# A rank-20 product for the second MLP matmul, with sixteen kept sums

## The chip, the cores and the metric

The program runs on one core of a Trainium2 chip. A core has TensorE (PE in the profile, its weight loads PEld), VectorE (DVE), ScalarE (ACT), GpSimd (POOL) and SyncE (SP, which here only starts transfers), each with its own in-order queue of instructions. The metric is device time in microseconds, the median of several runs.

## The reference

Four batches of 768 tokens pass a gated linear attention with 8 heads of width 48, then a two-layer MLP with an ELU. Everything is single precision for the kernel; the MLP weights arrive as 64-bit floats.

```python
f = 1.0 / (1.0 + np.exp(-f_logit))
for t in range(S):
    state = f[:, :, t, :, None] * state + np.einsum('bhd,bhe->bhde', k[:, :, t], v[:, :, t])
    y[:, :, t] = np.einsum('bhd,bhde->bhe', q[:, :, t], state)
x = y.transpose(0, 2, 1, 3).reshape(B * S, H * D)      # 3072 x 384
h = x @ w_in                                            # 384 x 2048
g = np.where(h > 0.0, h, np.exp(np.minimum(h, 0.0)) - 1.0)
out = g @ w_out                                         # 2048 x 384
```

## The kernel before

The 3072 tokens are cut into 12 units of 256 (two blocks of 128). The work of a unit in the MLP is 16 steps T (unit m has T = 16m to 16m+15); two steps make a pair P, and a pair handles 256 of the 2048 hidden features, so a unit has 8 pairs j = 0 to 7. The main loop writes out the order by hand, step by step, in the order in which it is then queued on every engine:

- At an even T, `up7` (L891 ff.) makes the first product for pair P. It saves one product in eight with sums of weights and inputs (`mix`, `blend`, both on GpSimd), and writes two banks of PSUM, `pa` and `pb`, which are one buffer each: the next pair's `pb` products cannot start before VectorE has read this pair's. Eight instructions go to `pa`, twelve to `pb`. Between the two groups ScalarE copies one block of `pa` (L908, `u1`), VectorE adds it to two others (L910, `hh`), and then VectorE does the ELU of the pair before (`elu`, L955).
- At an odd T, `joined` (L920 ff.) adds the rest from `pb` with three VectorE additions (L923), then ScalarE runs Relu and Exp over the 128x512 result (L933, L934).
- `elu(P)` runs two steps after `joined(P)`, and from its 128x512 result GpSimd makes four sums of 128x128 blocks (L965).
- At an odd T, `down(P-2)` (L969 ff.) multiplies with `w_out`. Here too seven products of half width (192 columns) replace eight, with four blocks of hidden values, four sums of them (`sums`), four blocks of `w_out` and four combinations of them made once (`combine`, L861 ff., VectorE, steps 16 to 31). They accumulate over the unit's 8 pairs in four PSUM banks m0 to m3. A single-precision matmul is two instructions in the trace, so a pair's second product is 14 instructions of 192 columns. When j = 7 is done, one ScalarE copy and five VectorE additions (L1013, L1014) turn the seven sums into the output, and SyncE stores it.
- Unit 0 does both products plainly, since the combinations are not ready: 8 instructions of 384 columns for a pair (L978).

The attention of later units lies between these steps, put there with `at_step`. For unit u it is, in steps counted from the start of unit u-1: at T = 2 transposes of k; at T = 5 `both(u)`, with products into banks a0, a1 and then scores into m3 and m0 (the step's `down` is left out and made up at T = 7), the masks (L721) and the state additions (L694) on VectorE; at T = 9 `outputs`; at T = 11 `carried`; at T = 13 `blend` on GpSimd. The gates of the unit after come at T = 9, 11, 13 and 15: a scan (L630) and a reciprocal (L635) on VectorE, products with k and q on GpSimd (L625).

The kernel also rereads the weights in 32 pieces during units 3 to 10 and checks their range (`check`, L601 ff.): two VectorE reductions (L607) for each, at T = 6, 10, 14 and 2. One small matmul group on bank m3 at T = 4 (16 matmuls) and one on a0 at T = 22 (5) are there for no result (`warm`).

Of the kernel before, what the change touches and what calls it, by code (L numbers as in the profile page):

```python
# [8 lines left out]
FP32 = mybir.dt.float32  # L9
# [4 lines left out]
ALU = mybir.AluOpType  # L14
# [339 lines left out]


@with_exitstack
def fast(ctx: ExitStack, tc: tile.TileContext, q, k, v, f_logit, w_in, w_out, out, flag, outer):
# [33 lines left out]
    NP = NFT // 2  # L391
    DH = DM // 2
    DIRECT = 1
    LAG = 2
    AHEAD = 7
    WA = 1
    F1 = 3
    W0 = 3
    SMALL = 16
    MORE = 5  # L400
    RR = 2
# [7 lines left out]
    MX = 10  # L409
    CB = 16  # L410
    BL1 = 13
    LIMIT = 2.0**80

    FULL = (slice(0, 64), slice(64, 128))
# [85 lines left out]

    even_v = cst.tile([128, NW, NKT, 64], FP32, name="even_v")
    nc.gpsimd.memset(even_v[:], 0.0)
    padded_v = cst.tile([128, NW, 2 * NKT, 3 * PAD], FP32, name="padded_v")
    nc.gpsimd.memset(padded_v[:], 0.0)
    padded_s = cst.tile([128, NC - 1, NKT, 3 * PAD], FP32, name="padded_s")
    nc.gpsimd.memset(padded_s[:], 0.0)
    between = cst.tile([128, NW, HP], FP32, name="between")
# [9 lines left out]
    if wide:  # L517
        combos = [area[:, i].bitcast(FP32).rearrange("p (n f) -> p n f", f=DH) for i in (5, 6, 0, 1)]
    else:
        apart = cst.tile([128, 4, NP, DH], FP32, name="combos")  # L520
        combos = [apart[:, i] for i in range(4)]

# [78 lines left out]
    def check(n):  # L601

        if not wide:
            return
        hi = again.pop(n)[:].bitcast(FP32)[:, 1::2]
        for i, op in enumerate((ALU.min, ALU.max)):
            nc.vector.tensor_reduce(  # L607
                out=spans[:, i, n : n + 1], in_=hi, axis=mybir.AxisListType.X, op=op, apply_absolute_value=True
            )

# [149 lines left out]
    def carried(u):  # L760
# [3 lines left out]
        for w in range(NW):  # L764
            for p in range(HP):
                for b in range(2):
# [3 lines left out]
                    for r in range(2):  # L770
# [4 lines left out]
                        )  # L775
        x = xts[u] = sb.tile([128, HP + 1, U], FP32, tag="xt", name=f"xt{u}", bufs=3)
        to = x[:, 0:HP].rearrange("n p (w b i) -> n b w p i", b=2, i=C)
# [9 lines left out]
    def first_outputs(part):  # L787
# [32 lines left out]
        if part == 0:  # L820
            for b in range(2):
                nc.scalar.copy(between[:, :, 0:NKT], first_y[b][:, :, :, 0])
            return
        x = xts[0] = sb.tile([128, HP + 1, U], FP32, tag="xt", name="xt0", bufs=3)
        to = x[:, 0:NKT].rearrange("n p (w b i) -> n b w p i", b=2, i=C)
# [6 lines left out]
    def at_step(step, *todo):  # L832
        plan.setdefault(step, []).extend(todo)
# [27 lines left out]
    def combine():  # L861

        b = [[wo[:, i::2, h * DH : (h + 1) * DH] for h in range(2)] for i in range(2)]
        t = combos
        for n in range(0, NP, 2):
            for to, x, y in (
                (t[0], b[0][1], b[0][0]), (t[1], b[1][1], t[0]), (t[2], b[1][1], b[0][1]), (t[3], b[1][0], t[1]),
            ):
                nc.vector.tensor_tensor(
                    out=to[:, n : n + 2], in0=x[:, n : n + 2], in1=y[:, n : n + 2], op=ALU.subtract  # L870
                )
                yield

# [78 lines left out]
    def elu(P):  # L952
        m, j = order[P]
        g = gs[P]
        nc.vector.scalar_tensor_tensor(  # L955
            out=g[:], in0=g[:], scalar=-1.0, in1=phs.pop(P), op0=ALU.add, op1=ALU.max
        )
        if m >= DIRECT:
            s = ss[P] = sb.tile([128, 4, 128], FP32, tag="sums", name=f"sums{m}_{j}", bufs=3)
            a = [[g[:, i, t * 128 : (t + 1) * 128] for i in range(2)] for t in range(2)]  # L960
            for i, x, y, op in (
                (0, a[1][0], a[1][1], ALU.add), (2, a[0][0], a[1][0], ALU.subtract),
                (1, s[:, 0], a[0][0], ALU.subtract), (3, a[0][1], s[:, 1], ALU.subtract),
            ):
                nc.gpsimd.tensor_tensor(out=s[:, i], in0=x, in1=y, op=op)  # L965

    left = []

    def down(P):  # L969
        m, j = order[P]  # L970
        if j == 0:
            pms[m] = [ps.tile([128, DM], FP32, tag=f"m{i + (m < DIRECT)}", name=f"psM{m}_{i}") for i in range(NW if m < DIRECT else 4)]
        pm, g = pms[m], gs.pop(P)
        ends = dict(start=(j == 0), stop=(j == NP - 1))
        if m < DIRECT:
            for i in range(2):
# [12 lines left out]
            return  # L989
        s = ss.pop(P)  # L990
        a = [[g[:, i, t * 128 : (t + 1) * 128] for i in range(2)] for t in range(2)]
        b = [[wo[:, 2 * j + i, h * DH : (h + 1) * DH] for h in range(2)] for i in range(2)]
        c = [combos[i][:, j] for i in range(4)]

        todo = [
            (0, 0, a[0][0], b[0][0]), (3, 0, a[0][1], b[1][0]), (0, 1, s[:, 1], c[1]),
            (1, 0, s[:, 0], c[0]), (1, 1, s[:, 2], c[2]), (2, 1, a[1][1], c[3]), (2, 0, s[:, 3], b[1][1]),
        ]
        if j == 0:
            todo = todo[3:] + todo[:3]  # L1000
        for bank, half, x, y in todo:
            first = j == 0 and (bank, half) in ((0, 0), (3, 0), (1, 0), (2, 1))
            nc.tensor.matmul(  # L1003
                pm[bank][:, half * DH : (half + 1) * DH], lhsT=x, rhs=y,
                start=first, stop=(j == NP - 1), skip_group_check=True,
            )
        if j == NP - 1:
            p = [[pm[i][:, h * DH : (h + 1) * DH] for h in range(2)] for i in range(4)]
            o = (outer if (NU - m) % 2 else sb).tile([128, 2, DM], FP32, tag="o", name=f"o{m}", bufs=1)
            u2 = sb.tile([128, DH], FP32, tag="u2", name=f"u2_{m}", bufs=1)  # L1010
            u43 = sb.tile([128, 2, DH], FP32, tag="u43", name=f"u43_{m}", bufs=1)
            flat = o[:].rearrange("p t f -> p (t f)")
            add = lambda to, x, y: nc.vector.tensor_tensor(out=to, in0=x, in1=y, op=ALU.add)  # L1013
            (nc.vector.tensor_copy if m == NU - 1 else nc.scalar.copy)(u2[:], p[0][0])  # L1014
            add(flat[:, 0:DH], p[3][0], u2[:])
            add(u2[:], p[0][1], u2[:])
            add(u43[:], pm[1][:].rearrange("p (h f) -> p h f", h=2), u2[:].unsqueeze(1).broadcast_to([128, 2, DH]))
            add(flat[:, 3 * DH :], p[1][0], u43[:, 1])
            add(flat[:, DH : 3 * DH], pm[2][:], u43[:].rearrange("p h f -> p (h f)"))
            def store(*queues):  # L1020
                for t in range(2):
                    for h in ((1, 0) if t else (0, 1)):
                        queues[t].dma_start(
                            out=out[m * U + t * 128 : m * U + (t + 1) * 128, h * DH : (h + 1) * DH],
                            in_=o[:, t, h * DH : (h + 1) * DH],
                        )

            if m == NU - 1:
                left.append(store)
            else:  # L1030
                store(nc.sync, nc.sync)
            del pms[m]

    low = cst.tile([128, 1], FP32, name="low")

    def finish_flag(part):
        if wide and not part:
            ok = fine[:, 0, 0:1]
            nc.vector.tensor_reduce(out=spans[:, 0, 0:1], in_=spans[:, 0], axis=mybir.AxisListType.X, op=ALU.min)
            nc.vector.tensor_reduce(out=spans[:, 1, 0:1], in_=spans[:, 1], axis=mybir.AxisListType.X, op=ALU.max)  # L1040
            for i, op, limit in ((0, ALU.is_ge, 1.125 * 2.0**-15), (1, ALU.is_lt, 1.875 * 2.0**16)):
                nc.vector.scalar_tensor_tensor(
                    out=ok, in0=spans[:, i, 0:1], scalar=limit, in1=ok, op0=op, op1=ALU.mult
                )
        if not part:
            nc.vector.tensor_reduce(
                out=low[:], in_=fine[:].rearrange("p a c -> p (a c)"), axis=mybir.AxisListType.X, op=ALU.min
            )
            return
        pf = ps.tile([128, 1], FP32, tag="a0", name="psF")  # L1050
        nc.tensor.matmul(pf[0:1, :], lhsT=low[:], rhs=causal[:, W - 1 : W], start=True, stop=True)
        nc.vector.tensor_copy(flag[:], pf[0:1, :])
# [97 lines left out]
    at_step(4, lambda: warm(0, "m3", SMALL))  # L1150
    at_step(22, lambda: warm(0, "a0", MORE))
    attention(1, (), A1)
# [3 lines left out]
    weights = combine()  # L1156
    for n in range(NFT):
        at_step(CB + n, lambda: next(weights))
# [17 lines left out]
    for T in range(NU * NFT):  # L1176
# [14 lines left out]
        for n in later.pop(T, ()):  # L1191
            split(n)
            if n not in (A1[2], A1[2] + 1):
                lower(n)
    elu(NU * NP - 1)
    for P in range(NU * NP - LAG, NU * NP):
# [51 lines left out]
```

## Time and profile before

| what | before |
|---|---|
| median of 3 runs | 562.21 us (561.53 to 562.24) |
| profiled execution, its own time | 563.12 us |
| its span from first to last instruction | 561.4 us |
| PE busy | 542.9 us, 97% |
| DVE busy | 407.5 us, 73% |
| POOL busy | 293.3 us, 52% |
| ACT busy | 228.1 us, 41% |
| one unit, 311.55 to 354.74 us | 43.19 us |

In the profile a group of instructions is a line of the kernel, an engine, an operation and its tiles; then come how often it ran, its busy time, the mean length of one, and the idle time of the engine just before it with what ended that. The time from one instruction's start to the next one's is less than the length of one, because instructions of an engine overlap at their ends.

### The profile page before, as it was taken

How to read it: one execution, taken by the hardware profiler on the slowest of the kernel's cores; microseconds unless marked ns; L12 is line 12 of the kernel's file. 1: busy time of each engine (PE TensorE's matmuls, PEld its weight loads, DVE VectorE, ACT ScalarE, POOL GpSimd, SP SyncE). 2: the span in 40 equal slices, each digit the busy share in tenths (PEclk: the TensorE clock that was granted, in tenths of full speed). 3: DMA queues.
4: the chain of work that ended last, by engine and by line, in shares of the span. 5: the costliest groups of instructions: out<-in, count | busy, mean ns of one | idle time of the engine just before them, and what ended most of it. 6: DMA issues, size and time to landing. Idle time of an engine off the chain costs nothing.

```text
span 561.4 us, 15627 instructions
## 1 busy us (share of the span) xinstructions
PE 542.9 (97%) x6358; PEld 507.9 (90%) x6358; DVE 407.5 (73%) x804; ACT 228.1 (41%) x442; POOL 293.3 (52%) x567
## 2 busy tenths in 40 slices
PE   6889989999999999999999999999999999999996
PEld 2466768999999999999999999999999999999995
DVE  8888989786675785785785785786687777735553
ACT  3288752443343434434344343343333343333331
POOL 6600797475375375465366267257258348325332
PEclk9999989999999999999999999999999999999999
DMA  8999971024025216207307307207307302301101
GB/s 198 233 266 247 276 184 43 3 48 123 2 48 149 61 26 182 77 18 189 81 9 189 87 10 190 85 9 191 86 9 185 93 9 71 87 5 33 31 2 34
DMA packets 39474, 54.30 MB, mean 97 GB/s; under 512 B 4032, under 2 KB 29216, under 8 KB 39392
## 3 DMA queue, kind: packets, MB, share of 16 engines
q1 hardware_dynamic: 38592, 52.61, 36.3%
q8 instruction: 52, 0.85, 0.6%
q10 hardware_dynamic: 800, 0.59, 0.5%
q14 instruction: 30, 0.25, 0.2%
HBM read 45.02 MB, written 4.72 MB: 89 GB/s over the span
## 4 chain that ended last, share of the span: by engine, by line
PE 85%; DMA 7%; DVE 3%; ACT 2%; issue 1%; SPq 1%; POOL 0%; ACTq 0%; DVEq 0%; POOLq 0%
PE psH L901 39%; PE psM L1003 36%; DMA area<-in_moe_w_in_dram 5%; DMA area<-in_moe_w_out_dram 2%; PE psY L751 2%; PE psY L771 2%; PE psU_a L736 2%; PE psS L713 2%; ACT area L577 1%; PE psT L673 1%; PE psM L978 1%; DVE bits L567 1%; DVE gg L955 0%; DVE wi L585 0%; DVE state L694 0%
## 5 line engine op out<-in xcount | busy, mean ns | idle before, releaser
L901 PE MATMUL psH<-xt,wi 128*128 128x128 f32 (+1 forms) x1056 | 195.9, 295 | 0.0
L965 POOL TENSOR_TENSOR sums<-gg 128x128 f32<-128x128 f32 x176 | 77.6, 462 | 209.6 <-DVE gg L955 190.9
L933 ACT ACTIVATE gg<-hh 128x512 f32<-128x512 f32 x88 | 55.5, 631 | 252.9 <-DVE hh L923 111.9
L901 PEld LDWEIGHTS psH<-xt,wi 128*128 128x128 f32 x1056 | 150.1, 192 | 1.6
L901 PE MATMUL psH<-xt,area 128*128 128x128 f32 x704 | 122.0, 275 | 2.0 <-DVE gg L955 2.0
L901 PEld LDWEIGHTS psH<-xt,area 128*128 128x128 f32 x704 | 106.9, 192 | 6.8 <-DVE gg L955 2.2
L910 DVE TENSOR_TENSOR hh<-psH,u 128x256 f32<-128x256 f32 x88 | 37.0, 421 | 99.6 <-ACT u L908 99.6
L1003 PE MATMUL psM<-area,sums 128*128 128x192 f32 x528 | 102.1, 326 | 0.1
L1003 PEld LDWEIGHTS psM<-area,sums 128*128 128x128 f32 x528 | 88.0, 190 | 0.2 <-issue 0.2
L1003 PE MATMUL psM<-wo,gg 128*128 128x192 f32 x352 | 73.9, 332 | 0.0
L955 DVE SCALAR_TENSOR_TENSOR gg<-gg,hh 128x512 f32<-128x512 f32 x88 | 63.3, 720 | 1.5 <-ACT gg L934 1.5
L635 DVE RECIPROCAL f<-f 128x256 f32<-128x256 f32 x36 | 62.8, 1747 | 1.1
L934 ACT ACTIVATE gg<-gg 128x512 f32<-128x512 f32 x96 | 60.5, 631 | 3.0
L1003 PEld LDWEIGHTS psM<-wo,gg 128*128 128x128 f32 x352 | 56.3, 190 | 1.4
L923 DVE TENSOR_TENSOR hh<-psH,u43h 128x256 f32<-128x256 f32 (+1 forms) x176 | 54.7, 353 | 3.0
L965 POOL TENSOR_TENSOR sums<-gg,sums 128x128 f32<-128x128 f32 x88 | 46.8, 532 | 6.9
L625 POOL TENSOR_TENSOR q<-q,f 128x256 f32<-128x256 f32 x48 | 39.7, 829 | 18.1 <-DMA area<-in_moe_w_in_dram 15.1
L625 POOL TENSOR_TENSOR k<-k,f 128x256 f32<-128x256 f32 x48 | 39.7, 830 | 9.5 <-DMA f<-f 6.7
L923 DVE TENSOR_TENSOR u43h<-psH,hh 128x256 f32<-128x256 f32 x88 | 37.0, 421 | 9.2 <-PE psH L901 8.5
L965 POOL TENSOR_TENSOR sums<-sums,gg 128x128 f32<-128x128 f32 x88 | 43.4, 493 | 0.0
L1003 PE MATMUL psM<-area,gg 128*128 128x192 f32 x176 | 43.0, 326 | 0.0
L1003 PE MATMUL psM<-wo,sums 128*128 128x192 f32 x176 | 43.0, 326 | 0.0
(100 smaller groups left out, 648.7 us busy)
## 6 DMA issues: line engine op xcount, KB each, us to landing
area<-in_moe_w_out_dram SPq DMA_DIRECT2D x8, 768.0 KB, 11.0
again<-in_moe_w_in_dram SPq DMA_DIRECT2D x16, 384.0 KB, 4.2
again<-in_moe_w_out_dram SPq DMA_DIRECT2D x16, 384.0 KB, 3.7
k<-in_k_dram SPq DMA_DIRECT2D x12, 384.0 KB, 4.5
q<-in_q_dram SPq DMA_DIRECT2D x12, 384.0 KB, 5.6
v<-in_v_dram SPq DMA_DIRECT2D x12, 384.0 KB, 6.0
area<-in_moe_w_in_dram SPq DMA_DIRECT2D x8, 576.0 KB, 9.4
out_dram<-o SPq DMA_DIRECT2D x42, 96.0 KB, 2.0
```

The lines of the kernel that those rows point to most:

```text
L625: e.tensor_tensor(out=t[n][:, p], in0=t[n][:, p], in1=t["f"][:, p, "kq".index(n)], op=ALU.mult)
L635: nc.vector.reciprocal(f[:, p, 1], f[:, p, 0])
L713: nc.tensor.matmul(pc[r][FULL[b], w, p], lhsT=t["k"][FULL[r], p, cols], rhs=t["q"][FULL[r], p, cols], start=True, stop=True,)
L736: nc.tensor.matmul(pu[b][FULL[r], w, p], lhsT=kn[FULL[b], p, w, FULL[r]], rhs=vs[u % NB][FULL[b], w, PAD + h * D : PAD + (h + 1) * D], sta ...
L901: nc.tensor.matmul(to, lhsT=lhs, rhs=rhs, start=(n == 0), stop=True, skip_group_check=True)
L910: add = lambda to, x, y: nc.vector.tensor_tensor(out=to, in0=x, in1=y, op=ALU.add)
L923: add = lambda to, x, y: nc.vector.tensor_tensor(out=to, in0=x, in1=y, op=ALU.add)
L933: nc.scalar.activation(g[:], h, AF.Relu, scale=-1.0)
L934: nc.scalar.activation(g[:], g[:], AF.Exp, scale=-1.0)
L955: nc.vector.scalar_tensor_tensor(out=g[:], in0=g[:], scalar=-1.0, in1=phs.pop(P), op0=ALU.add, op1=ALU.max)
L965: nc.gpsimd.tensor_tensor(out=s[:, i], in0=x, in1=y, op=op)
L1003: nc.tensor.matmul(pm[bank][:, half * DH : (half + 1) * DH], lhsT=x, rhs=y, start=first, stop=(j == NP - 1), skip_group_check=True,)
```

## The change

The second product for two pairs (four tiles of 128 hidden features, two token blocks, three column blocks of 128) is made with 20 products of 128 columns in place of 2 times 7 of 192. The 20 products go to 16 sums c0 to c15, four to a PSUM bank. They need 14 sums of hidden blocks a0 to a13 and 14 combinations b0 to b13 of weight blocks. Names in the tables: x0 to x7 are hidden blocks (4 features tiles by 2 token blocks), w0 to w11 blocks of `w_out`, o0 to o5 blocks of the output.

- `elu`: after an even pair GpSimd makes a0 to a3 (4 additions); after an odd pair VectorE makes a5, a7, a10 (3), and GpSimd the other 8.
- `down`: an even pair issues the first 10 products, an odd pair the other 10. In the last unit the last two pairs' 20 are issued together, by bank.
- `ended`: after a unit ScalarE copies three banks (128x512 each) and one block of the fourth, and VectorE does 22 additions of 128x128. They are put out four at the end of each step (`SPREAD`), from step 3 of the next unit; the store follows. In the last unit they run at once, four of them on GpSimd.
- `combine`: 20 operations of 128x512, 18 on GpSimd and 2 on VectorE, at steps 18 to 37.
- Unit 1 does its second product plainly.
- `check`: Square and Relu on ScalarE with their row sums, in place of the two VectorE reductions.
- Smaller: the group of 5 `warm` matmuls goes and the other has 15; three padded tiles become one (`spare`), cleared by one instruction; the MLP inputs have two buffers in place of three.

```diff
-    SMALL = 16
-    MORE = 5
+    PLAIN = 2
+    SPREAD = 4
+    SMALL = 15
-    CB = 16
+    CB = 18
...
+SUMS_OF_TWO = table(
+    "a0 x0 - x1, a1 a0 - x4, a2 x5 + a1, a3 x0 - x4, "
+)
+SUMS_SOON = table(
+    "a5 x2 - x6, a7 x4 + x2, a10 x2 - x7, "
+)
+SUMS_OF_FOUR = table(
+    "a12 a0 + x7, a4 x6 - x7, a6 x5 + a4, a9 x4 + x6, a8 x1 + x2, a8 a8 - x3, a13 x0 + x2, a11 x3 - x7, "
+)
+PRODUCTS = (
+    table(
+        "x4 b10 c0, x5 w5 c11, x1 b12 c14, a0 b1 c2, a1 b8 c1, a2 w3 c8, a3 b6 c7, x7 b9 c10, x2 b5 c4, "
+        "a5 w6 c9, "
+    ),
+    table(
+        "a7 b3 c3, a10 b4 c5, a12 b7 c6, a4 b13 c11, a6 b0 c15, a9 b11 c15, a8 w11 c14, a8 w10 c13, "
+        "a13 b2 c13, a11 w9 c12, "
+    ),
+)
+OUTPUTS = table(
+    "o0 c7 + c12, o1 c3 - c13, o2 c7 - c14, c1 c0 + c1, c2 c2 - c1, c4 c3 - c4, c5 c5 + c4, c6 c6 - c2, "
+    "c8 c8 - c6, c9 c9 - c5, o0 o0 + c10, o0 o0 + c5, o0 o0 - c6, o1 o1 + c7, o1 o1 + c2, o2 o2 + c4, "
+    "o2 o2 - c1, o3 c10 + c8, o3 o3 - c9, o5 c11 - c0, o5 o5 - c9, o4 c8 - c15, "
+)
...
-        for i, op in enumerate((ALU.min, ALU.max)):
-            nc.vector.tensor_reduce(
-                out=spans[:, i, n : n + 1], in_=hi, axis=mybir.AxisListType.X, op=op, apply_absolute_value=True
-            )
+        nc.scalar.activation(hi, hi, AF.Square, accum_out=spans[:, 0, n : n + 1])
+        nc.scalar.activation(hi, hi, AF.Relu, bias=1.0, scale=-SMALLEST, accum_out=spans[:, 1, n : n + 1])
...
+        if m < PLAIN:
+            return
+        Q = P // 2
+        if P % 2 == 0:
+            ss[Q] = sb.tile([128, 14, 128], FP32, tag="sums", name=f"sums{m}_{j // 2}")
+        for engine, rows in ((nc.gpsimd, SUMS_OF_TWO),) if P % 2 == 0 else (
+            (nc.vector, SUMS_SOON), (nc.gpsimd, SUMS_OF_FOUR)
+        ):
+            for row in rows:
+                combined(engine, lambda name: hidden(Q, name), row)
...
+        whole = m == NU - 1 and j >= NP - 2
+        if whole and j == NP - 2:
+            return
+        todo = PRODUCTS[j % 2]
+        if whole:
+            todo = sorted(PRODUCTS[0] + PRODUCTS[1], key=lambda row: int(row[2][1:]) // 4)
+        for x, y, c in todo:
+            bank, at = divmod(int(c[1:]), 4)
+            nc.tensor.matmul(
+                pm[bank][:, at], lhsT=hidden(Q, x), rhs=weight(j // 2, y),
+                start=bank not in begun, stop=(j == NP - 1), skip_group_check=True,
+            )
...
+    def ended(m):
+        for b in range(3):
+            nc.scalar.copy(kept[:, 4 * b : 4 * b + 4], pm[b][:])
+        last = spare[:, NQ * 128 : (NQ + 1) * 128]
+        nc.scalar.copy(last, pm[3][:, 3])
...
+        if m < NU - 1:
+            pending.extend(lambda row=row: combined(nc.vector, at, row) for row in OUTPUTS)
+            pending.append(lambda: store(nc.sync, nc.sync))
+            return
+        for row in OUTPUTS_AT_THE_END:
+            combined(nc.gpsimd if row[0] in ("o3", "o5") else nc.vector, at, row)
+        left.append(store)
...
+        for f in pending[:SPREAD]:
+            f()
+        del pending[:SPREAD]
```

## The prediction

> **What bounds the kernel now.** I read the busy shares first, then the chain of waits in order of time, then two timelines. The busy shares and the costliest groups:
>
> ```profile
> PE 542.9 (97%) x6358; PEld 507.9 (90%) x6358; DVE 407.5 (73%) x804; ACT 228.1 (41%) x442; POOL 293.3 (52%) x567
> ...
> L607 DVE TENSOR_REDUCE spans<-again 128x1 f32<-128x384 f32 x64 | 31.3, 531 | 0.0
> ...
> L978 PE MATMUL psM<-wo,gg 128*128 128x384 f32 x64 | 22.6, 497 | 0.0
> ```
>
> TensorE is the bound: it idles 18.5 us in all, 5.8 of them after its last product (555.6) and nearly all others before unit 1. The other queues only have to be on time. The chain gives the price of each kind of PE work without the overlap at its ends:
>
> ```profile
> 83.84 2.44 PE psH L901 x20
> 86.28 2.58 PE psM L978 x8
> ...
> 122.03 2.28 PE psM L1003 x14
> ...
> 362.00 2.44 PE psH L901 x20
> ```
>
> Fourteen instructions of 192 columns take 2.28 us, eight of 384 take 2.58. A first product is 18 instructions of 128 columns and 2 of 256, so 22 times 128 columns in 2.44 us: 0.111 us for 128 columns. The windows show one unit, 311.55 to 354.74 us: 43.19 us, in which PE never stops and VectorE is busy 32.05, ScalarE 16.63, GpSimd 23.39.
>
> How much time the others have is read where VectorE is busiest, the joint step (T = 5) and what leads to it. The timelines of VectorE and PE there:
>
> ```profile
> 350.81 0.36 DVE L1013 TENSOR_TENSOR o<-psM,u 128x192 f32<-128x192 f32 x1 [1.62 <-ACT u L1014]
> ...
> 353.06 0.41 DVE L910 TENSOR_TENSOR hh<-psH,u 128x256 f32<-128x256 f32 x1
> 353.39 0.68 DVE L955 SCALAR_TENSOR_TENSOR gg<-gg,hh 128x512 f32<-128x512 f32 x1
> 353.99 0.42 DVE L923 TENSOR_TENSOR u43h<-psH,hh 128x256 f32<-128x256 f32 x1
> 354.45 0.62 DVE L923 TENSOR_TENSOR hh<-psH,u43h 128x256 f32<-128x256 f32 x2
> 354.98 1.28 DVE L721 TENSOR_TENSOR at<-psS,twice 128x512 f32<-128x512 f32 x2
> ```
>
> ```profile
> 354.74 0.49 PE L901 MATMUL psH<-xt,wi 128*128 128x128 f32 x2
> ```
>
> PE starts pair j = 3's first product at 354.74. Its ninth instruction, the first into `pb`, comes 8 x 0.111 later, at 355.63, and may not start before the three L923 additions of pair 2 have read that bank. They end at 355.07. So the slack here is **0.56 us**.
>
> The last view is GpSimd and VectorE together at 111.7 to 113.5 us:
>
> ```profile
> 111.75 0.55 DVE L869 TENSOR_TENSOR area<-wo,area 128x384 f32<-128x384 f32 x1
> 111.82 0.80 POOL L965 TENSOR_TENSOR sums<-sums,gg 128x128 f32<-128x128 f32 x1
> 112.22 0.95 DVE L630 TENSOR_TENSOR_SCAN f<-f 128x256 f32<-128x256 f32 x1
> 112.70 0.72 POOL L965 TENSOR_TENSOR sums<-gg,sums 128x128 f32<-128x128 f32 x1
> ```
>
> An L965 sum alone takes 0.46, a scan alone 0.68. Here they take turns: the sum takes 0.34 longer (until the combination is through), the scan 0.26 longer (until that sum is), the next sum 0.26 longer. VectorE operations with an operand in PSUM (L910, L923, L721) show no such lengthening in the rows where GpSimd runs beside them. From these numbers a 128x128 sum on GpSimd holds VectorE's two-SBUF-operand operations for about 0.32, and one of those of 128 columns holds GpSimd for about 0.14 (0.41 for 384 columns, by thirds). A round of one each is 0.46, against 0.20 from start to start on VectorE alone (two L923 operations and the L721 behind them). The Trainium skill (GPSIMD Engine Reference, Specifications) says that GpSimd's SBUF interface is shared with VectorE instructions that have two SBUF inputs; it gives no price.
>
> **The change, part by part.** The profiled execution took 563.12 us by its own time (span 561.4 and 1.7 around it), 0.9 over the median of the runs, 562.21. Sums are made on 563.12.
>
> *Products.* For each pair of units 2 to 11, 14 instructions of 192 columns (2.28) become 20 of 128 (2.22 to 2.24 at 0.111 to 0.112). Gain 0.045 x 80 pairs = **-3.6 us**, all on the path. Unit 1 done plainly: (2.58 - 2.28) x 8 = **+2.4**. Twelve fewer small `warm` instructions: 42 of them are busy 1.3 us, so **-0.3** (bounds 0 and -0.4).
>
> *Range checks.* Each check takes 1.0 us from VectorE (2 x 0.53) and gives ScalarE two operations of 384 columns. The nearest rows are a 384-column copy at 0.47 and Relu of 512 at 0.63, so 1.0 to 1.2 together; the row sum is not shown by any row, and I bound it by 0 and 0.16 each (a copy of 8 columns). They stand at T = 2, 6, 10, 14, ahead of the `u1` copy. At T = 2 the chain `u1`, L910, ELU, L923 has 0.23 us to spare (L923 waited that long for PE, at 348.10), so the joint chain comes 0.8 later. The changed kernel's instruction order holds one load of tables on ScalarE, as before, where the trace has one of 1.28 us, so I add nothing for it. The Trainium skill (ScalarE: Activation LUTs, Table sets) speaks against mixing functions here: a switch to another table set costs about 2.7 us, and Square is not in its list of what comes with Exp. By that page, with 64 switches, the sum would be an estimated 173 us more, about 784; no row of this trace shows a switch.
>
> *Output sums, copies and the joint step.* Each unit from 2 on now ends with three 128x512 copies and one of 128x128 on ScalarE, and VectorE's five L1013 operations (2.18) become 22 additions, 4 a step. With the times of the trace of before: Exp ends at 350.57; the copies start 0.48 apart (as the kn copies do), end at 352.3, and `u1` is done at 352.5, not 351.5. L910 and the ELU then run to 353.6. Between that ELU and L923 now stand seven additions with both operands in SBUF (a5, a7, a10 and four output sums). The same ELU releases GpSimd's eight sums, so they run side by side. Alone, seven take 7 x 0.20 and 0.2 for those that wait on each other: 1.6. Taking turns, 7 x 0.46 = 3.2. L923 adds 1.1, and the check's delay 0.8: `pb` is free at 357.1 or 358.7 against 355.63. PE waits **1.4 or 3.1 us**. I take 3.1: the alternation is what the nearest rows show, whenever both engines had such work. This is once in each of units 3 to 10.
>
> *The rest of the unit.* VectorE's queue: 32.05 less 3.90 (checks) and 2.18, plus 34 additions of 0.28, is 35.5; some 20 of them run beside GpSimd (+0.26 each, 5.2), and ELUs meet it too (up to +0.34, as at 337.94; say 1.4). That is 42 of 43 us, so the queue does not catch up. Next place: T = 8 to 10. From PE's start of step 8, Exp ends at 2.1, the two gate activations (0.83, 0.84) at 3.6, `u1` 3.8, L910 and ELU 4.8, five additions in turns 7.1, L923 8.2; PE wants `pb` after 2.44 + 1.09 (outputs) + 2.23 + 0.89 = 6.65. About 1.4 us. The other two places where an ELU is followed by additions (T = 12 and 0, with a check on ScalarE near) I put at 0.6 each. Together **2.6** (bounds 0 and 3.6).
>
> *GpSimd* makes 12 sums for two pairs in place of 8: +1.8 us of 9.4, and 18 combinations of 512 columns (about 1.27 each from 0.46 and 0.73 for 128 and 256). The combinations lie in steps 18 to 37 beside the k and q products and are needed at step 39. **+0.4** (0 to 3). After T = 12 its queue (8 sums, 5 blends, k, q, 4 sums) has just the time to the product of j = 6; what it lacks is in the next rival.
>
> *Unit 11* has the additions but no joint step: **+1.5** (0 to 4).
>
> *Tail.* Before, PE ends at 555.6 and the last addition at 557.3. After, c3 waits for a7, which follows the last ELU (552.35) by 0.9; 34 instructions of 0.111 then end at 557.0. The third bank is copied at 556.1, and 13 dependent additions from there, four more on GpSimd beside them, end near 559.5. **+2.2** (0.9 to 3). The store waits on the last.
>
> *Covered:* one clear of 1392 columns for three on GpSimd, before PE's work begins; two input buffers in place of three, since unit u's are written when unit u - 2 is long through; the store, now behind step 8 on SyncE, with rereads behind it that wait 4 steps anyway. If any cover fails it costs under 1 us.
>
> Sum: 8 x (3.1 + 2.6) = 45.6, - 3.6 + 2.4 - 0.3 + 0.4 + 1.5 + 2.2 = +48.2 us: 563.1 + 48.2 = 611.3, or on the median **611**.
>
> **Rivals.**
> 1. *No turns for such short operations* (the rows show them for 256 to 512 columns). Then the joint step costs 1.4, the rest 0.4: 8 x 1.8 = 14.4, with the other terms (2.0) 16: about 579. For it: the stalls need many short operations in a row. Against it: a 128x3 operation took 0.41 for 0.15 at 125.09.
> 2. *PE stays the bound* (the other side). L923 would have to end before 355.63, which decides: more than 0.56 us late and the gain of 0.36 a unit is gone. Then -3.6 + 2.4 - 0.3 and a hidden tail: about 560.7. Against it: even without turns and without the checks' delay I find L923 0.7 too late.
> 3. *GpSimd becomes a second bound* after T = 12, its sums late for `down` by 1 to 2 us a unit: about 623.
>
> **How the numbers follow.** Likeliest (turns, 595 to 618): 0.50. Rival 1 and between (566 to 595): 0.24. Rival 3 (618 to 635): 0.13. Rival 2: 0.13, of it 0.02 within 0.2%. Two tenths of a per cent is about what a measurement tells from no change. So slower 0.87, same 0.02, faster 0.11. The range leaves out rival 2 and the far end of rival 3: 567 to 629; the likeliest's own is 595 to 618.
>
> **What would show it.** In the profile after: PE idle before L956 (the first product) released by VectorE, some 3 us once a unit after the joint scores, and units of 48 to 49 us; 128x128 additions on VectorE at 0.45 and more where GpSimd sums; psM groups of 20 in 2.23 us; PE's busy share well under 97%. Wrong if units still take 43 us (rival 2) or 45 (rival 1).

## The result and the profile after

The changed kernel takes **629.12 us** (median of 4 runs, 628.32 to 631.5) against 561.87 on the same chip (4 runs): a ratio of 1.1209, 95% interval 1.1173 to 1.1246. It is 67 us slower. The forecast was slower, 611 us, with a range that ended at 629; the time lies 0.1 us beyond it. The profiled execution took 629.21 us by its own time, with a span of 627.5.

From the page of the kernel after, the busy shares, the granted clock in 40 slices, and the costliest group of waiting matmuls (busy us and mean ns, then the idle time before them with its releaser):

```profile
PE 568.0 (91%) x6778; PEld 516.7 (82%) x6778; DVE 460.5 (73%) x1006; ACT 277.3 (44%) x602; POOL 382.0 (61%) x715
...
PEclk9998999999999998997997997999999899899898
...
L956 PE MATMUL psH<-xt,area 128*128 128x128 f32 x704 | 128.4, 286 | 33.5 <-DVE hh L978 32.9
```

TensorE's share fell from 97 to 91%, and its matmuls into `pb` (L956, the old L901) now wait 32.9 us for VectorE's L978 (the old L923). Its busy time rose by 25 us, though the products are cheaper. The row of clocks shows most of the reason: from the middle on nearly every third slice is at 0.7 or 0.8, where before one slice in all was below 0.9.

The products cost what was forecast. The timeline of PE at one pair, after:

```profile
425.00 0.83 PE L1079 MATMUL psM<-area,sums 128*128 128x128 f32 x6
...
427.01 0.39 PE L1079 MATMUL psM<-wo,sums 128*128 128x128 f32 x2
427.24 0.39 PE L956 MATMUL psH<-xt,wi 128*128 128x128 f32 x2
```

Twenty instructions from 425.00 to 427.24: 2.24 us, against 2.28 for the fourteen before.

One unit in the windows (length; busy us of PE, PEld, VectorE, ScalarE, GpSimd; granted clock; DMA share; GB/s), after:

```profile
421.91:472.49 50.58, 45.94 (x569) 43.73 (x568) 37.79 (x88) 22.48 (x56) 31.36 (x62) 0.97 0.31 80
```

50.58 us in place of 43.19. No engine but PE (and its weight loads) is busy more than 38 of them, which points to order and not to the sum of work; the experiments test it. The joint step of that unit (the timeline of all engines, lines of weight loads and of other work left out):

```profile
429.87 1.54 ACT L1097 COPY kept<-psM 128x512 f32<-128x512 f32 x3
...
431.29 0.29 ACT L1099 COPY spare<-psM 128x128 f32<-128x128 f32 x1
...
431.44 0.30 ACT L963 COPY u<-psH 128x128 f32<-128x128 f32 x1
431.61 0.68 DVE L1026 TENSOR_TENSOR o<-kept,psM 128x128 f32<-128x128 f32 x3 [3.04 <-ACT spare L1099]
432.21 0.28 DVE L1026 TENSOR_TENSOR kept<-kept 128x128 f32<-128x128 f32 x1
432.41 0.42 DVE L965 TENSOR_TENSOR hh<-psH,u 128x256 f32<-128x256 f32 x1
432.75 0.68 DVE L1010 SCALAR_TENSOR_TENSOR gg<-gg,hh 128x512 f32<-128x512 f32 x1
...
433.46 0.29 DVE L1026 TENSOR_TENSOR sums<-gg 128x128 f32<-128x128 f32 x1
433.51 0.56 POOL L1026 TENSOR_TENSOR sums<-sums,gg 128x128 f32<-128x128 f32 x1 [3.84 <-DVE gg L1010]
433.67 0.55 DVE L1026 TENSOR_TENSOR sums<-gg,gg 128x128 f32<-128x128 f32 x1
434.03 0.50 POOL L1026 TENSOR_TENSOR sums<-gg 128x128 f32<-128x128 f32 x1
434.14 0.54 DVE L1026 TENSOR_TENSOR sums<-gg 128x128 f32<-128x128 f32 x1
434.60 1.66 DVE L1026 TENSOR_TENSOR kept<-kept 128x128 f32<-128x128 f32 x4
...
436.19 0.41 DVE L978 TENSOR_TENSOR u43h<-psH,hh 128x256 f32<-128x256 f32 x1
...
437.40 0.98 PE L956 MATMUL psH<-xt,area 128*128 128x128 f32 x3 [3.36 <-DVE hh L978]
```

This is the chain that the prediction named: kept copies ahead of `u1`, then L965, the ELU, seven additions that take turns with GpSimd's sums (2.73 us, from 433.46 to 436.19; 0.21 to 0.57 from start to start, with five of GpSimd's sums begun between them), then L978, and PE waits 3.36 us. In units 4 to 10 it is 3.36 every time, in unit 3, where the checks only begin, 2.08; together 25.6 of the 32.9 us. One thing in it was not named. Four output additions stand *ahead* of L965; they wait for the last kept copy, and hold L965 back by 0.67 us after `u1` is done (431.74 to 432.41).

At the end of each wait of 3.36 us the granted clock goes to 0.5 for 3.41 or 6.83 us (437.04 to 440.45 in this unit), which costs PE 1.7 or 3.4 us of work. In the unit from 371.00 it was 6.83 us long.

Where the 66.1 us of span came from, by places on PE (us against before; the forecast's terms added up the same way, with the 0.36 of cheaper products in each unit; units from their T = 2 to the next):

| place | forecast | measured |
|---|---|---|
| up to the second product for the second pair of unit 1 | +0.4 | -1.4 |
| from there to T = 2 of unit 2, six plain pairs (32.49 to 33.48) | +1.8 | +1.0 |
| unit 2, with the last plain pair (43.18 to 43.41) | 0.0 | +0.2 |
| units 3 to 9 (302.3 to 351.0) | +37.4 | +48.7 |
| unit 10 (42.5 to 48.5) | +5.3 | +6.0 |
| unit 11 up to its last pair (28.9 to 34.2) | +1.1 | +5.3 |
| from there to the end (14.9 to 21.2) | +2.2 | +6.3 |

### The profile page after: what moved, and what is told of

Its sections match the earlier page's. It is cut to its first block, busy times and chain, and to the rows that moved or that the text cites. A ratio compares the mean times of both kernels' runs of the same rounds, so it can differ in the third digit from the quotient of the medians.

```text
span 627.5 us, 16865 instructions
## 1 busy us (share of the span) xinstructions
PE 568.0 (91%) x6778; PEld 516.7 (82%) x6778; DVE 460.5 (73%) x1006; ACT 277.3 (44%) x602; POOL 382.0 (61%) x715
## 5 line engine op out<-in xcount | busy, mean ns | idle before, releaser
L956 PE MATMUL psH<-xt,wi 128*128 128x128 f32 (+1 forms) x1056 | 201.6, 301 | 2.5 <-DVE hh L965 2.5
L956 PE MATMUL psH<-xt,area 128*128 128x128 f32 x704 | 128.4, 286 | 33.5 <-DVE hh L978 32.9
L956 PEld LDWEIGHTS psH<-xt,wi 128*128 128x128 f32 x1056 | 151.5, 197 | 5.8 <-DVE hh L965 3.4
L956 PEld LDWEIGHTS psH<-xt,area 128*128 128x128 f32 x704 | 110.8, 198 | 42.9 <-issue 29.1
L1026 POOL TENSOR_TENSOR sums<-sums,gg 128x128 f32<-128x128 f32 x120 | 62.2, 518 | 101.9 <-DVE gg L1010 95.7
L1026 POOL TENSOR_TENSOR sums<-gg 128x128 f32<-128x128 f32 x160 | 75.9, 474 | 73.5 <-DVE gg L1010 69.1
L1079 PE MATMUL psM<-area,sums 128*128 128x128 f32 x720 | 117.5, 282 | 1.2 <-DVE sums L1026 1.2
L965 DVE TENSOR_TENSOR hh<-psH,u 128x256 f32<-128x256 f32 x88 | 37.0, 420 | 107.7 <-ACT u L963 107.6
L1079 PEld LDWEIGHTS psM<-area,sums 128*128 128x128 f32 x720 | 99.2, 197 | 3.3 <-DVE sums L1026 1.4
L1079 PE MATMUL psM<-wo,sums 128*128 128x128 f32 x400 | 72.1, 278 | 0.0
L1079 PE MATMUL psM<-area,gg 128*128 128x128 f32 x320 | 59.4, 289 | 0.6 <-DVE o L1026 0.5
L1079 PEld LDWEIGHTS psM<-wo,sums 128*128 128x128 f32 x400 | 58.1, 194 | 0.9
L1026 POOL TENSOR_TENSOR sums<-gg,gg 128x128 f32<-128x128 f32 x120 | 57.6, 493 | 0.0
L978 DVE TENSOR_TENSOR hh<-psH,u43h 128x256 f32<-128x256 f32 (+1 forms) x176 | 54.7, 353 | 3.0
L1079 PEld LDWEIGHTS psM<-area,gg 128*128 128x128 f32 x320 | 48.1, 201 | 1.9 <-ACT u L963 0.7
L1026 POOL TENSOR_TENSOR sums<-gg,sums 128x128 f32<-128x128 f32 x80 | 43.6, 544 | 6.3
```

The lines of the kernel that those rows point to most:

```text
L956: nc.tensor.matmul(to, lhsT=lhs, rhs=rhs, start=(n == 0), stop=True, skip_group_check=True)
L1026: engine.tensor_tensor(out=at(to), in0=at(x), in1=at(y), op=ALU.add if sign == "+" else ALU.subtract)
L1079: nc.tensor.matmul(pm[bank][:, at], lhsT=hidden(Q, x), rhs=weight(j // 2, y), start=bank not in begun, stop=(j == NP - 1), skip_group_chec ...
```

## The experiments

In what follows a difference of two runs is that of their medians; the kernel before ran at 562.3 to 564.0 beside them, so a difference between runs of different numbers below is good to 2 or 3 us, and the ratios carry the intervals.

Theories to tell apart: the loss is the one burst of additions in the joint chain; it is the turns with GpSimd; VectorE's queue as a whole is too full; the halved clock is the part that was not foreseen.

### 1. Without GpSimd's sums: what the turns cost

```diff
+            if engine is nc.gpsimd:
+                continue
             for row in rows:
                 combined(engine, lambda name: hidden(Q, name), row)
...
```

The rest of the edit, in `hidden`, gives the products plain blocks in place of the sums that are left out, so what is stored is not the result.

> The changed kernel without GpSimd's twelve sums for two pairs; the products read plain hidden blocks in their place (a5, a7, a10 are still made), so those sums are left out of the computation. Theory 1, taking turns (a two-operand addition on VectorE waits for the GpSimd sum in front of it): the seven additions before L978 go from 0.47 to 0.20 or 0.32 apart, the wait of PE at the joint step from 3.4 to about 2 us, no halved clock after it, units of 45 us: 580 to 592. Theory 2, the queue of VectorE is too long with or without GpSimd: the wait stays above 3 us, 615 to 629.

Measured: 599.68 us, ratio 1.0654 (1.0624 to 1.0684), between the two forecasts; units 4 to 10 take 46.5 to 48.8 us, and the clock still halves in five of them. Timelines of VectorE and PE in a joint step:

```profile
370.61 0.29 DVE L1028 TENSOR_TENSOR sums<-gg 128x128 f32<-128x128 f32 x1
370.82 0.28 DVE L1028 TENSOR_TENSOR sums<-gg,gg 128x128 f32<-128x128 f32 x1
371.02 0.28 DVE L1028 TENSOR_TENSOR sums<-gg 128x128 f32<-128x128 f32 x1
371.23 1.01 DVE L1028 TENSOR_TENSOR kept<-kept 128x128 f32<-128x128 f32 x4
372.16 0.42 DVE L978 TENSOR_TENSOR u43h<-psH,hh 128x256 f32<-128x256 f32 x1
...
373.38 0.98 PE L956 MATMUL psH<-xt,area 128*128 128x128 f32 x3 [2.18 <-DVE hh L978]
```

The same seven additions take 1.55 us, not 2.73, and PE's wait is 2.18, not 3.36: the turns are worth 1.18 us of it, to the hundredth. With GpSimd's sums 29 of the 67 us go. That is nearly all the turns: the weight loads of the changed kernel wait only 1.3 us in all for a late sum of GpSimd. The other 2.18 us of the wait needs no GpSimd.

### 2. Fewer output additions, none in the joint step

Of the 22 output additions in units 2 to 10 only 6 are made (`OUTPUTS_FEW`, not shown), three at T = 3 and the others from T = 7; what is stored is not the result.

```diff
-            pending.extend(lambda row=row: combined(nc.vector, at, row) for row in OUTPUTS)
+            pending.extend(lambda row=row: combined(nc.vector, at, row) for row in OUTPUTS_FEW)
...
-        for f in pending[:SPREAD]:
+        now = 3 if T % 16 == 3 else SPREAD if T % 16 > 6 else 0
+        for f in pending[:now]:
```

> The changed kernel with 6 of the 22 output additions of units 2 to 10 (16 left out, so the stored values are not the products): three at step 3, where they read PSUM, three from step 7. The four between the ELU of step 4 and L978 are gone. If the burst there is what costs: the wait 3.4 less 4 x 0.47 and 0.2, about 1.3 us, no halved clock, units of 44.5 to 45.5: 578 to 592. If the checks on ScalarE and the copies carry it: over 605.

Measured: 590.91 us, ratio 1.0503 (1.0479 to 1.0528), at the upper end of the first forecast; the joint wait is 1.8 to 1.9 us, and units 4 to 10 take 45.0 to 47.4. The 16 additions and the place of the others carry 38 of the 67 us, but a wait of nearly 2 us stays, with three additions ahead of L965 and the three hidden sums the only ones left in the chain. What else could make it, the copies and the check ahead of `u1`, is tried in 6.

### 3. The same additions at odd steps only

```diff
+        now = SPREAD if T % 2 else 0
-        for f in pending[:SPREAD]:
+        for f in pending[:now]:
             f()
-        del pending[:SPREAD]
+        del pending[:now]
```

> The changed kernel with the output additions put out only at the end of odd steps (four each, steps 3 to 13), none between an ELU and L978. All work is done. If their place is what costs: three additions stay in front of L978, the wait falls by 4 x 0.47 to about 1.5 us, no halved clock: 585 to 600. If it is their number, because VectorE is busy all round the unit: the wait moves to steps 8 to 14, 610 to 629.

Measured: 603.32 us, ratio 1.0713 (1.0677 to 1.0749), a little above what "place" forecast; PE's joint wait is 1.77, and the clock still halves in four units. All the work is there, and 26 us of the 67 are gone. Leaving out 16 additions as well, in experiment 2, gave 12 more: where the additions stand counts for more here than how many they are.

### 4. The checks back on VectorE

```diff
-        nc.scalar.activation(hi, hi, AF.Square, accum_out=spans[:, 0, n : n + 1])
-        nc.scalar.activation(hi, hi, AF.Relu, bias=1.0, scale=-SMALLEST, accum_out=spans[:, 1, n : n + 1])
+        for i, op in enumerate((ALU.min, ALU.max)):
+            nc.vector.tensor_reduce(
+                out=spans[:, i, n : n + 1], in_=hi, axis=mybir.AxisListType.X, op=op, apply_absolute_value=True
+            )
...
```

> The changed kernel with the range checks back on VectorE. If the 1.4 us that the check takes of ScalarE at step 2 sits on the joint chain: L978 comes some 0.9 us sooner, the wait falls from 3.4 to 2.4, and the 1 us of VectorE is paid behind the state additions where it is needed less: 612 to 622. If VectorE's queue is full all round the unit, the 4 us a unit that come back to it cost more than that: 629 to 650.

Measured: 632.4 us, ratio 1.1246 (1.1222 to 1.1269), 2 to 3 us above the changed kernel and within the second forecast. The wait for L978 (L980 in this run) stays at 3.4 to 3.5 us, and small ones for VectorE come on top:

```profile
PE psH L958 <- DVE hh L980: 32.9, 19, 3.5
...
PE psH L958 <- DVE fine L706: 3.5, 7, 0.5
```

So the 1.0 us per check is missed on VectorE about as much as it is on ScalarE ahead of `u1`.

### 5. PE's wait filled with work for nothing: is the halved clock on the path?

```diff
     joint = [(u - 1) * NFT + A3[1] for u in range(3, NU)]
+    for t in joint[1:]:
+        at_step(t + 1, lambda: warm(3, "m1"))
```

> The changed kernel, with three matmuls of 512 columns into bank m1 for no result at T = 6 of units 3 to 10, so that PE works through most of its 3.36 us wait; all of the kernel's own work is done. Theory A (the granted clock of 0.5 after each long wait costs PE 1.7 or 3.4 us a unit, and that is on the path): no stretch at 0.5 in the units, periods of 47 to 49 us in place of 50.5, 602 to 617 us. Theory B (VectorE's queue is full and sets the period by itself, and the halved clock only fills time in which PE would wait): periods stay at 50 to 50.9, 625 to 633 us.

Measured: 625.37 us, ratio 1.1094 (1.1048 to 1.114): the time is theory B's. Its row of clocks and one unit in its windows:

```profile
PEclk9998999999999999999999999999999999999898
```

```profile
421.28:471.84 50.56, 47.41 (x574) 43.67 (x573) 37.75 (x88) 22.49 (x56) 31.30 (x62) 1.00 0.30 81
```

The clock stays at 1.00 through units 3 to 10, the unit still takes 50.56 us. Follow one unit by the start of each first product, counted from its T = 2 (after, from 320.37, with the clock at 0.5 for 6.83 us; then this run, from 321.18):

| | `pb` at T = 6 | T = 8 | T = 10 | T = 12 | T = 14 | T = 0 | next T = 2 |
|---|---|---|---|---|---|---|---|
| after | 15.49 | 24.26 | 30.22 | 36.19 | 40.86 | 45.54 | 50.63 |
| filled | 15.50 | 21.59 | 27.60 | 34.71 | 39.73 | 45.15 | 50.46 |

The 2.7 us of dummy work change nothing at T = 6, so it is VectorE that lets PE go on. At full speed PE is 2.7 us ahead at T = 8, and has lost 2.5 of them again by T = 2. A place where it loses some of them shows in PE's timeline:

```profile
348.78 0.39 PE L956 MATMUL psH<-xt,wi 128*128 128x128 f32 x2
349.00 0.39 PE L956 MATMUL psH<-xt,area 128*128 128x128 f32 x2
349.23 0.61 PE L956 MATMUL psH<-xt,wi 128*128 128x128 f32 x4
350.75 0.68 PE L956 MATMUL psH<-xt,area 128*128 128x128 f32 x4 [0.91 <-DVE hh L978]
```

That is the wait at T = 10 that the prediction named. The profile after has it in unit 3 alone (0.91 at 199.18), the one of these units where the clock stayed at full speed; in units 4 to 10 PE came there later by the slow clock. So the theory that the halved clock is the part that was not foreseen falls: it lies mostly in time that PE would have waited. The kernel after shows the same by itself: the unit from 320.37 has 6.83 us of half clock and takes 50.63, the one from 421.91 has 3.41 and takes 50.58. In units 3 to 10 the two traces differ by 3.2 us (399.5 to 396.3), the two ratios by 6.5 of 67. Theory B has the pace right but not its reason, for VectorE's queue is not full. Its waits in the unit from 321.18:

```profile
DVE hh L965 <- ACT u L963: 8.6, 6, 3.8
DVE o L1026 <- ACT spare L1099: 3.0, 1, 3.0
```

It is busy 38.03 of the unit's 50.46 us and waits 11.6 for ScalarE. That leaves the chain through both engines (checks, copies, `u1`, L965, ELU, additions, L978) to set the pace, not either's sum of work; the next experiment shortens it by order alone.

### 6. Copies, checks, and all three edits of order

Copies behind `u1` (`late` is emptied after `up` of the even step):

```diff
-            ended(m)
+            if m < NU - 1:
+                late.append(lambda: ended(m))
+            else:
+                ended(m)
...
         if T % 2 == 0:
             up(P)
+            while late:
+                late.pop(0)()
```

> The changed kernel, with a unit's four kept copies queued on ScalarE behind the u1 copy of the joint step, not ahead of it. Theory A (the joint chain Exp, copies, u1, L965, ELU, seven additions, L978 sets the wait): u1 and all behind it come 1.0 to 1.7 us earlier, the joint wait falls from 3.36 to 1.7 to 2.4 us, the clock halves less often, 600 to 618 us. Theory B (the time VectorE lacks comes out at the next place): the joint wait falls but others grow by as much, 624 to 632 us.

Measured: 611.78 us, ratio 1.0858 (1.0819 to 1.0897), theory A's time, and the clock never halves in the units. PE waits for L978 in a joint step, and two pairs later at T = 10:

```profile
231.16 0.68 PE L956 MATMUL psH<-xt,area 128*128 128x128 f32 x4 [0.88 <-DVE hh L978]
...
245.69 0.68 PE L956 MATMUL psH<-xt,area 128*128 128x128 f32 x4 [1.42 <-DVE hh L978]
```

The joint wait falls from 3.36 to 0.9 us, further than theory A said, and 1.4 or 1.8 us come out at T = 10 instead, which is theory B's part in it.

The same run shows what the turns depend on. Here the first four output additions, three of which read PSUM, come behind the ELU and beside GpSimd's sums (timelines of GpSimd and VectorE):

```profile
229.01 0.45 POOL L1026 TENSOR_TENSOR sums<-gg,sums 128x128 f32<-128x128 f32 x1
229.01 0.67 DVE L1026 TENSOR_TENSOR o<-kept,psM 128x128 f32<-128x128 f32 x3
229.60 0.43 DVE L1026 TENSOR_TENSOR kept<-kept 128x128 f32<-128x128 f32 x1
```

The three take 0.67 together, as without GpSimd beside them (0.68 at 431.61 in the kernel after), and the next one, with both operands in SBUF, is long again. All 27 additions of this run with an operand in PSUM and GpSimd beside them take 0.28 each; the 224 with both operands in SBUF and GpSimd beside them take 0.44 on average.

Checks behind `u1`:

```diff
-        at_step(t + 4, lambda n=n: check(n))
+        behind[t + 4] = lambda n=n: check(n)
...
             down(P - LAG)
+        if T in behind:
+            behind[T]()
```

> The changed kernel, with the range checks queued on ScalarE behind the first product's u1 copy, not ahead of it. Theory A (the check at T = 2 delays the joint chain by 0.8 us, as the prediction has it): the joint wait falls from 3.36 to about 2.5 us, 612 to 624 us. Theory B (the chain has room for it, or VectorE is full): the wait stays within 0.2 us of 3.36 and the time within 626 to 632 us.

Measured: 606.02 us, ratio 1.0737 (1.0694 to 1.078), better than theory A's 612 to 624; the joint wait is 2.1 us. A check is at T = 2, 6, 10 and 14, each with its 1.36 us ahead of a `u1`; I had priced only the one at T = 2.

All three:

> The changed kernel with three edits of order: output additions only at odd steps, kept copies behind the joint step's u1, range checks behind u1. All work is done. Theory A (place and order, not the amount of VectorE's work, make the loss): odd steps alone left a joint wait of 1.8 us; the copies take 1.0 to 1.7 off it and the checks 0.8, so it goes, and with it the halved clock: units of 43.2 to 44.8 us and 572 to 588 us. Theory B (VectorE has too much work beside GpSimd for a period of 43 us): units of 45 and more, 592 to 605 us.

Measured: 588.07 us, ratio 1.0412 (1.0366 to 1.0459), at the very end of theory A's range, with units 3 to 9 at 44.7 to 45.8 us, longer than the 43.2 to 44.8 that it said. The waits of PE (total, times, longest):

```profile
PE psM L1079 <- DVE o L1026: 7.8, 8, 1.5
...
PE psH L956 <- DVE hh L978: 2.5, 7, 0.4
```

Without a single instruction less, 41 of the 67 us are gone, by order alone. Singly the three edits gave 26, 17 and 23 us, 66 in all: they shorten the same chain, so their gains do not add up. The wait for `pb` went from 32.9 to 2.5 us. A new wait of 0.6 to 1.5 us a unit stands before the third product of T = 7, the one that opens the fourth bank of PSUM: the three additions that still read it come later now.

### 7. What is left of it

The run with all three edits, less GpSimd's 12 sums (as in 1):

> The run odd_and_both_behind (588 us) with GpSimd's 12 sums for two pairs left out: the products read the plain blocks x0 and x1 in their place. VectorE's work is all done. Theory A (turns between VectorE's and GpSimd's operations are what is left of the loss): units of 43.0 to 43.6 us, 562 to 571 us. Theory B (the count of VectorE's operations and their place are what is left): units of 44.4 and more, 577 to 588 us.

Measured: 575.53 us, ratio 1.0221 (1.0192 to 1.0249), between the two, units of 43.5 to 44.8. In this order the turns cost 12.5 us, not 29. Of the 13 us that are left, 5.3 are the tail, 1.5 unit 11 and 6.0 units 3 to 9, by the same places as in the table; what makes these 6.0 was not tried.

The same run with all sums, the product that opens the fourth bank put last of its ten, and all last stores on SyncE:

```diff
-        "x4 b10 c0, x5 w5 c11, x1 b12 c14, a0 b1 c2, a1 b8 c1, a2 w3 c8, a3 b6 c7, x7 b9 c10, x2 b5 c4, "
-        "a5 w6 c9, "
+        "x4 b10 c0, x5 w5 c11, a0 b1 c2, a1 b8 c1, a2 w3 c8, a3 b6 c7, x7 b9 c10, x2 b5 c4, "
+        "a5 w6 c9, x1 b12 c14, "
...
-            store(nc.sync, nc.scalar)
+            store(nc.sync, nc.sync)
```

> The run odd_and_both_behind with two edits: in the first table of products the one that opens the fourth bank (x1 b12 c14) comes last of the ten and not third, and the last stores are all started by SyncE. All work is done. Theory A (the wait of 0.6 to 1.5 us a unit that was left before that product is for the output additions that still read the fourth bank): it goes, units of 43.8 to 44.8 us, and with the tail 572 to 582 us. Theory B (the wait only moves to the next place): units of 44.7 to 45.7 us as before, 583 to 588 us.

Measured: 581.02 us, ratio 1.0338 (1.0312 to 1.0363), in theory A's range, but only partly for its reason: the wait for the fourth bank is gone, yet units take 44.4 to 45.3 us and PE waits up to 0.5 us for L978 again. Unit 11 is down to 29.4 us (28.9 before). This is the best version with all the work, still 19 us behind the kernel before.

### 8. The tail

The ends of the changed kernel, and of the one with all last stores on SyncE (timeline; SPq and ACTq are transfers):

```diff
-            store(nc.sync, nc.scalar)
+            store(nc.sync, nc.sync)
```

```profile
619.76 0.28 DVE L1026 TENSOR_TENSOR o<-o,psM 128x128 f32<-128x128 f32 x1
620.06 0.81 SPq L1110 DMA_DIRECT2D out_dram<-o  x2
620.42 3.91 ACTq L1110 DMA_DIRECT2D out_dram<-o  x2
```

```profile
619.90 0.28 DVE L1026 TENSOR_TENSOR o<-o,psM 128x128 f32<-128x128 f32 x1
620.20 2.69 SPq L1110 DMA_DIRECT2D out_dram<-o  x4
```

> The changed kernel, with the last unit's stores all started by SyncE, none by ScalarE. Theory A (in the tail, ScalarE comes late to the branch ahead of the stores, and its first store then takes 3.4 us to issue): from the start of the last first product to the end of the span 17.5 to 19 us in place of 21.2, and 625 to 627 us in all. Theory B (the first transfer behind the branch is slow on whichever queue): 20.5 to 21.5 us there, 628 to 631 in all.

Measured: 627.36 us, ratio 1.1154 (1.1133 to 1.1175); from the last first product to the end 19.06 us in place of 21.19, both just beyond the end of theory A's ranges and short of theory B's. In the kernel before, ScalarE's two stores took 0.92 us to issue, in the changed kernel 3.91, the first alone 3.39. That it is ScalarE's transfer is shown; why it is slow there (the engine comes to the branch late, behind its last kept copy at 617.4) was only argued. The four stores on one queue then follow each other (2.69 us), so not all of the 3 us comes back.

### 9. The checks alone, on the kernel before

```diff
-        for i, op in enumerate((ALU.min, ALU.max)):
-            nc.vector.tensor_reduce(
-                out=spans[:, i, n : n + 1], in_=hi, axis=mybir.AxisListType.X, op=op, apply_absolute_value=True
-            )
+        nc.scalar.activation(hi, hi, AF.Square, accum_out=spans[:, 0, n : n + 1])
+        nc.scalar.activation(hi, hi, AF.Relu, bias=1.0, scale=-SMALLEST, accum_out=spans[:, 1, n : n + 1])
...
```

> The kernel before, with only the range checks changed as the change has them (Square and Relu on ScalarE in place of two VectorE reductions). Theory A (checks on ScalarE are hidden as long as TensorE is the bound, with no reload of tables): 560.5 to 563 us, units of 43.2 us. Theory B (the 1.36 us on ScalarE ahead of u1 use up the 0.23 us that the chain has to spare, and L923 comes 0.2 to 0.6 us too late in each of 8 units): 563.5 to 568 us.

Measured: 565.15 us, ratio 1.0054 (1.0035 to 1.0073): theory B, a small loss but clear of the noise. One unit in the windows:

```profile
300.86:344.40 43.54, 43.42 (x535) 42.28 (x534) 28.57 (x59) 21.18 (x53) 23.37 (x46) 1.00 0.36 92
```

VectorE has 3.5 us less to do and the unit is 0.36 us *longer*, all of it in the joint step's pair (2.89 us in place of 2.54 from its first product to the next group). That is the prediction's step, and nearly its number: with 0.56 of slack and 0.36 of wait L923 comes 0.9 late, where the prediction had 0.8.

## Why the prediction was right, and where it was wrong

*Right.* The sign, the place of the longest wait, its mechanism and the engine. Products: 2.22 to 2.24 forecast, 2.24 measured. The check's delay: 0.8 forecast, 0.9 by experiment 9. The joint wait: 3.1 forecast, 3.36 measured, and that near a hit is partly luck. The seven additions in turns take 2.73 us, not 3.2, because not every one meets a sum: the turns are worth 1.18 us of the wait by experiment 1, not 1.7. Against that stand the 0.67 us by which the four output additions hold L965 back, which the sum did not have. A check's length: 1.36 us, within the 1.0 to 1.5 of its bounds; of it 0.41 are the two row sums, instructions of their own (ScalarE's timeline, after):

```profile
425.02 0.59 ACT L658 ACTIVATE again<-again 128x384 f32<-128x384 f32 x1
425.47 0.23 ACT L658 ACTIVATION_READ_ACCUMULATOR again<-again 128x1 f32 x1
425.73 0.56 ACT L659 ACTIVATE again<-again 128x384 f32<-128x384 f32 x1
426.20 0.18 ACT L659 ACTIVATION_READ_ACCUMULATOR again<-again 128x1 f32 x1
```

The trace has one load of tables on ScalarE, of 1.28 us at its start, and none between Square, Relu and the copies beside them. So the price of a switch in the Trainium skill (ScalarE: Activation LUTs, Table sets), from which the prediction estimated about 784 us, does not bear on this use of Square.

*Wrong: "The rest of the unit ... Together 2.6".* This term was the one that failed by size. A unit of 3 to 9 is 48.7 / 7 = 6.96 us longer; with the 0.36 that the products give, 7.3 are lost. The joint wait is 3.2 of them on average (3.36, but 2.08 in unit 3; forecast 3.1), so 4.1 are lost elsewhere (forecast 2.6). Over units 3 to 10 that is 12 of the 18 us missing (48.7 + 6.0 against 37.4 + 5.3). The step behind it was a full queue: VectorE's load put at 42 of 43 us, and the lag then priced at three places one by one. VectorE is busy 38 of 50.5 us and idle 11.6 for ScalarE (experiment 5), so the load was put too high and was not the cause. The runs show in its place that the chain through ScalarE and VectorE sets the pace nearly all the way from T = 5 to the next T = 2: when PE is given 2.7 us (experiment 5), they are gone within the unit. Two causes stand in the order of the code, and I passed over them. The four additions of step 3 stand ahead of L965 and wait for the kept copies, so VectorE idles 3.0 us there. And the checks at T = 6, 10 and 14 stand ahead of a `u1` as the one at T = 2 does (moving all four behind `u1` gave 23 us, where the joint step alone would give 1.3 x 8, about 10). How much of the 4.1 us each of the two makes is not separated, for the gains overlap.

*Wrong: "Unit 11 ... +1.5 (0 to 4)".* 5.3 by the table, where the forecast is 1.1. It has no joint step, but the same four and four additions around L965 and the ELU; PE waits 2.05 us there, and the clock halves again. With the additions at odd steps unit 11 loses 1.6.

*Wrong: "Tail ... +2.2 (0.9 to 3)".* From the last ELU to the last addition 7.86 us, 4.94 before: +2.9, within the bounds. The other 3.4 stand behind the last addition, in the stores: "The store waits on the last" was priced at nothing, and ScalarE's two took 3.91 us to issue in place of 0.92.

*The rest:* the stages up to unit 1 and the six plain pairs were 1.4 us shorter and 1.0 longer, not 0.4 and 1.8 longer. The plain products cost 2.58 us each, as forecast. The 1.4 is not shown to come from the change: the pair that starts at 98.24 in the kernel after starts between 97.6 and 101.2 in the runs above that share its code up to there. Two slips of the sums: on the median the sum is 611.3 less 0.9, so 610.4, not 611; and rival 1's other terms add up to 2.6, not 2.0.

*The rivals.* No turns (579): excluded by 1. PE stays the bound (560.7): excluded by the result. GpSimd as a second bound (623): the time is near, by luck, and the reason is not there; the weight loads wait 1.3 us in all, in eight places, for GpSimd's sums in the kernel after.

## What to carry to other kernels

When a chain through the helping engines sets the pace of a loop, price that chain for the whole period and not place by place: time that TensorE alone wins at one place is lost at the next (2.7 us won and 2.5 lost in experiment 5), and a slow clock on it costs little (3 to 6 of 67 us). Look at what stands *ahead* of a short copy that others wait for; here three moves of order, with no work removed, were worth 41 us. Even so no order tried here let a saving of 3.6 us on TensorE pay for 22 small additions a unit on an engine beside it; the best stayed 19 us behind. Small operations on VectorE with both operands in SBUF should not meet GpSimd's sums; with one operand in PSUM they met them here at no cost.

## What was not expected of the hardware

- The granted clock halves at a wait of PE, for 3.41 or 6.83 us. At the waits of 3.36 it did so every time, at 2.18 in five of seven units of experiment 1, at 2.1 in one of nine (checks behind `u1`), at 1.77 in four of seven (experiment 3) and in two of six (experiment 2), and at the five of 1.83 at T = 10 with the copies behind `u1` never. The steps of the clock lie on a grid: those of the kernel after are at 235.66, 283.44, 334.64 and 385.84 us, and so on, 14 or 15 times 3.413 us apart, so my reading, which no run tests, is that a wait counts by how it falls on that grid. The Trainium skill (TensorE: Matmul & The Clock Gate, What's actually happening) states a half-rate clock after an idle window of about 3.4 us, and that the window runs free; the lengths agree, but waits shorter than a window, down to 1.77 us, were enough here.
- The turns appear at 128 columns as well: over the whole kernel the 336 additions on VectorE take 126 us with GpSimd's sums beside them and 92 without (the groups of L1026 and L1028 added up). They need both operands in SBUF: 0.44 us on average against 0.28 with one in PSUM (experiment 6).
- ScalarE's first transfer behind the branch took 3.39 us to issue, 0.40 in the kernel before.
